# One evacuation path of an attention kernel: VectorE's two PSUM banks used one by one, batches of two units, and more than half of the integer shifts moved to GpSimd

## The chip, the cores and the metric

The kernel runs on one core of one Trainium2 chip. The metric is device time in microseconds (us) of one execution. The kernel before was timed at 739.3 us (median of three runs, 736.5 to 740.5).

Engine names in the profile: PE is TensorE (PEld its weight loads), ACT is ScalarE, DVE is VectorE, POOL is GpSimd, SP is the engine that issues most of the DMAs.

## The reference

Two attention blocks on the same input, mixed by a gate. Block A is softmax attention with 32 heads of 16 columns over 2048 positions; block B is linear attention.

```python
# B=1, S=2048, D=512, H=32, Dh=16
def _A_ref(x, wqkv, wo):
    q, k, v = ...                                    # (x @ wqkv), split in heads
    scores = jnp.einsum("bhqd,bhkd->bhqk", q, k) * (Dh ** -0.5)
    p = _softmax(scores, axis=-1)
    o = jnp.einsum("bhqk,bhkd->bhqd", p, v)
    return merge_heads(o) @ wo
g = sigmoid((x * gate_w).sum(-1, keepdims=True))
return g * _A_ref(x, A_wqkv, A_wo) + (1 - g) * _B_ref(x, B_wqkv, B_wo)
```

The cost is in A: 32 heads x 2048 x 2048 scores, each exponentiated once. In the kernel a *unit* is 128 keys x 512 queries of one head, and there are 2048 units to exponentiate (730 x 2 by ScalarE and 294 x 2 by VectorE in the kernel before).

## The kernel before

A scheduler written in Python lays out the instructions of all engines at build time, from a cost in nanoseconds that each operation is given. The order on each engine is then fixed. Engines are synchronised by semaphores where data demands it, and only there.

A unit's scores are exponentiated in one of two ways. ScalarE does it with one exponential for two units (128x1024). VectorE does it by arithmetic on the bits: it adds a constant to the scaled score, stores it as int16 (`op1`), and reads those bits as bfloat16, which is roughly a power of two. To be accurate enough it needs three such terms: the bits, the bits + 43 and the bits + 86 (`shift`), which TensorE sums with values scaled by three coefficients. TensorE's matmuls write to PSUM, here one tile, `ps`, of 4096 fp32 columns, which the kernel divides in eight banks of 512. Banks 0 to 3 hold scores for ScalarE, banks 4 and 5 those for VectorE, bank 7 the accumulator.

```python
SHIFTS = (0, 43, 86)
NPS, NZ, NQZ, NVQ = 10, 8, 3, 6
P = SB([128, NPS, 1024], BF16, "P")          # ScalarE's exponentials
Z = SB([128, NZ, 2048], I16, "Z")            # VectorE's, four units to a slot
# ... cut ...
def d_choose(start, late=0.0):               # may TensorE fill VectorE's banks now?
    if d_busy[0] or max(t_free(4), t_free(5)) > max(start + 30.0, late):
        return []                            # both banks have to be free
    # ... picks up to two units, for banks 4 and 5 ...

def cand_op1():                              # VectorE: both banks at once, 128x1024
    # ... cut ...
    return C(DV, 400, 533 * n + 74, lambda: nc.vector.tensor_scalar(o, i, ZB, 0.0, op0=ALU.add, op1=ALU.max), ...)

def cand_shift():                            # VectorE: four units at once, 128x2048
    # ... cut ...
    return C(DV, 300, 602, lambda: nc.vector.tensor_scalar(Z[:, z, :], Z[:, z0, :], float(m), None, op0=ALU.add), ...)

def cand_exp():                              # ScalarE: two units, 128x1024
    # ... cut ...
    return C(AC, 500, 427 * n + 49, lambda: nc.scalar.activation(P[:, slot, 0:512 * n], bank(b0, n), ACT.Exp, scale=ESC), ...)
```

GpSimd does small work. Its `tensor_scalar` operations are written so:

```python
# values times a coefficient, 32 times
nc.gpsimd.tensor_scalar(Vc[:, k, vs]..., Vc[:, 0, vs]..., COEF[k], 1.0, op0=ALU.mult, op1=ALU.mult)
# linear attention's feature map, 32 times each
nc.gpsimd.tensor_scalar(eb[:, i, :], eb[:, i, :], 1.0, 0.0, op0=ALU.min, op1=ALU.max)
nc.gpsimd.tensor_tensor(dst_ap, eb[:, i, :], mb[:, i, :], ALU.add)
# the gate, once each, on 64 columns
nc.gpsimd.tensor_scalar(ge[:], gt[:], 1.0, None, op0=ALU.add)                       # line 896
nc.gpsimd.tensor_scalar(ge[:], gt[:], -1.0, 1.0, op0=ALU.mult, op1=ALU.add)         # line 898
```

The main loop takes the candidate that can start first, appends it to its engine's list with the waits for its data (`emit`), and advances the planned clock.

The softmax here doesn't subtract the row's maximum and nothing guards it: scores larger than these inputs give would overflow.

Of the kernel before, what the change touches and what calls it, by code (L numbers as in the profile page):

```python
# [14 lines left out]
STATS = {}  # L15
# [110 lines left out]
def bass_gated_mix__mha_block__linear_attn_block__prompt_kernel(  # L126
# [31 lines left out]
    FILL = 0.65  # L158
    SLK = 0.0
# [3 lines left out]
    NPS, NZ, NQZ, NVQ = 10, 8, 3, 6  # L163

    with ExitStack() as es:
# [34 lines left out]
        Z = SB([128, NZ, 2048], I16, "Z")  # L200
# [225 lines left out]
        d_busy = [False]  # L426
# [71 lines left out]
        def d_batch():  # L498

            if dst["cur"] is None:  # L500
# [8 lines left out]
                dst["cur"] = {"todo": [0, 1, 2, 3], "z": z, "units": {}, "done": 0}  # L509
            return dst["cur"]  # L510

        def d_choose(start, late=0.0):

            if d_busy[0] or max(t_free(4), t_free(5)) > max(start + 30.0, late):
                return []
            cur = d_batch()
            if cur is None:
                return []
            js = sorted(cur["todo"], key=lambda j: (head(j), -len(uq[min(head(j), NR - 1)][j])))
            got = [(j, d_unit(j)) for j in js]  # L520
            got = sorted([x for x in got if x[1] is not None][:2])
            return [(cur, j, u, 4 + k) for k, (j, u) in enumerate(got)]
# [5 lines left out]
        class C:  # L528
            __slots__ = ("E", "prio", "dur", "fns", "reads", "writes", "after", "name", "mode", "wt")

            def __init__(self, E, prio, dur, fns, reads, writes, after, name, mode=None, wt=1.0):
                self.wt = wt
                self.E, self.prio, self.dur, self.fns = E, prio, dur, fns
                self.reads, self.writes, self.after, self.name, self.mode = reads, writes, after, name, mode

        def d_loaded(extra):
            for cur, j, u, bk in extra:
                r, kb = u
                take(r, kb, j)
                cur["todo"].remove(j)  # L540
                cur["units"][j] = u
                left[r][j] += NTERM - 1
                kb_left[(r, kb)] += NTERM - 1
            if extra:
                d_busy[0] = True
                dst["op1"].append((cur, [x[1] for x in extra]))
# [3 lines left out]
        def cand_s():  # L550
# [6 lines left out]
            extra = d_choose(start, s_window()[1] - SLK)  # L557
            units = act_pick(2, {x[1] for x in extra})
# [11 lines left out]
            def after(fin):  # L570
# [4 lines left out]
                STATS["sn"][nn] = STATS["sn"].get(nn, 0) + 1  # L575
                exps.append((sset, units))
# [20 lines left out]
        def cand_op1():  # L597
            if not dst["op1"]:
                return None
            cur, js = dst["op1"][0]  # L600
            z = cur["z"]
            n = len(js)

            def after(fin):
                dst["op1"].popleft()
                d_busy[0] = False
                cur["done"] += n
                d_finish(cur)
            zj = Z[:, z, :].rearrange("p (j c) -> p j c", j=4)
            o = zj[:, js[0]:js[1] + 1:js[1] - js[0], :] if n == 2 else zj[:, js[0], :]  # L610
            i = bank(4, 2).rearrange("p (j c) -> p j c", j=2) if n == 2 else bank(4)
            return C(DV, 400, 533 * n + 74, lambda: nc.vector.tensor_scalar(o, i, ZB, 0.0, op0=ALU.add, op1=ALU.max),  # L612
                     [r_bank[4 + k] for k in range(n)], [r_Z[z]], after, f"op1 {[cur['units'][j] + (j,) for j in js]}")

        def z_items(cur, z, term):
            for j, (r, kb) in cur["units"].items():
                def rel():
                    z_pend[z] -= 1
                add_item(r, kb, j, Z[:, z, 512 * j:512 * (j + 1)].bitcast(BF16), r_Z[z], rel, term, f"z{term}")

        def d_finish(cur):
            n = len(cur["units"])
            if cur["done"] < n or (cur["todo"] and any(d_unit(j) is not None for j in cur["todo"])) or cur.get("fin"):
                return
            if cur["todo"]:
                if any(head(j) < NR - 1 for j in cur["todo"]):
# [5 lines left out]
            z_pend[z] = n + NTERM - 1  # L632
            z_items(cur, z, 0)
# [3 lines left out]
        def cand_shift():  # L637
# [10 lines left out]
            cur, m, z0, kt = dst["shifts"][0]  # L648

            def after(fin):  # L650
# [3 lines left out]
                z_items(cur, z, kt)  # L654
            return C(DV, 300, 602, lambda: nc.vector.tensor_scalar(Z[:, z, :], Z[:, z0, :], float(m), None, op0=ALU.add),  # L655
                     [r_Z[z0]], [r_Z[z]], after, f"shift {m}")
# [708 lines left out]
```

## Time and profile before

| | before |
|---|---|
| span of the profiled run | 740.2 us |
| ScalarE busy | 697.7 us (94%), idle 42.5 |
| VectorE busy | 667.6 us (90%) |
| GpSimd busy | 128.3 us (17%) |
| granted TensorE clock | 0.977 |

The first line is the busy line of the page: us, share of the span, number of instructions.

```profile
PE 689.5 (93%) x6663; PEld 209.2 (28%) x6757; DVE 667.6 (90%) x813; ACT 697.7 (94%) x769; POOL 128.3 (17%) x184
```

These are groups of the page of the kernel before: line, engine, operation, tiles, shapes, count, then busy us and mean ns of one, then the idle time of the engine just before them and what ended it.

```profile
L677 ACT ACTIVATE P<-ps 128x1024 bf16<-128x1024 f32 x730 | 682.4, 1045 | 23.3 <-PE ps L331 22.1
L612 DVE TENSOR_SCALAR Z<-ps 128x1024 int16<-128x1024 f32 x294 | 357.2, 1215 | 42.8 <-PE ps L331 41.8
L655 DVE TENSOR_SCALAR Z<-Z 128x2048 int16<-128x2048 int16 x294 | 215.4, 750 | 3.0
...
L947 POOL TENSOR_SCALAR eb<-eb 128x512 f32<-128x512 f32 x32 | 23.1, 722 | 148.9 <-DVE mb L945 74.8
...
L876 POOL TENSOR_SCALAR Vc<-Vc 128x576 bf16<-128x576 bf16 x32 | 23.3, 727 | 88.6 <-DVE Vc L873 87.3
```

ScalarE's exponentials overlap (mean 1.045 us, but 682.4 / 730 = 0.935 us each), and it waits for TensorE only 22 us. The table by stretches of the span (columns: stretch, its length, then busy us of PE, PEld, DVE, ACT, POOL, then the granted clock and DMA) says that ScalarE is nearly full in the middle:

```profile
40.00:140.00 100.00, 94.25 (x908) 27.04 (x920) 95.70 (x119) 98.20 (x110) 23.27 (x31) 1.00 0.03 7
140.00:280.00 140.00, 131.33 (x1287) 39.18 (x1303) 130.49 (x152) 137.22 (x154) 31.36 (x40) 1.00 0.02 4
280.00:380.00 100.00, 96.85 (x961) 27.63 (x975) 91.94 (x112) 99.87 (x110) 7.54 (x14) 1.00 0.02 4
```

VectorE's shifts, in the view of one line's instructions (durations min/median/max in ns), are mostly alike, with a long tail:

```profile
L655 DVE TENSOR_SCALAR Z<-Z x294: 621/685/1754, 14.1 to 725.3; 128x2048 int16<-128x2048 int16 x147
```

And two lines of GpSimd's timeline (start us, duration us), the two gate operations quoted above.

```profile
67.72 0.87 POOL L896 TENSOR_SCALAR ge<-gt 128x64 f32<-128x64 f32 x1 [0.81 <-ACT gt L895]
69.26 0.24 POOL L898 TENSOR_SCALAR ge<-gt 128x64 f32<-128x64 f32 x1 [0.67 <-DVE gt L897]
```

The same 64 columns took 0.87 us with one operation and 0.24 us with two.

### The profile page before, as it was taken

What the parts mean: (1) busy time and instruction counts of PE and PEld (TensorE: products, weight loads), DVE (VectorE), ACT (ScalarE), POOL (GpSimd) and SP (SyncE); (2) the same over time, 40 slices, a digit from 0 to 9 for tenths busy, and PEclk for the clock granted to TensorE, in tenths of its full rate; (3) what the DMA queues carried; (4) which work ended last, traced back from release to release, by engine and by line L of the source; (5) the groups of instructions that cost most, each with busy time, mean ns of one, the idle gap of its engine ahead of it and who ended that gap; (6) DMA issues with size and microseconds to landing.
All of it is one profiled execution on the core that took longest, in us unless ns stands there. A gap on an engine that the chain in (4) does not pass through costs nothing.

```text
span 740.2 us, 16623 instructions
## 1 busy us (share of the span) xinstructions
PE 689.5 (93%) x6663; PEld 209.2 (28%) x6757; DVE 667.6 (90%) x813; ACT 697.7 (94%) x769; POOL 128.3 (17%) x184
## 2 busy tenths in 40 slices
PE   6999999899999999999999999999899989999997
PEld 2322222222323222222233322222233222222222
DVE  6799999998999999988897999999999968999894
ACT  4899999999999999999999999999999969999993
POOL 1301341212311220000010034233430000000000
PEclk8999999999999999999999999999999869999999
DMA  5900000000000000000000000000002021000001
GB/s 128 317 13 15 2 5 4 2 8 2 1 8 3 8 1 2 8 2 8 1 8 3 7 3 3 7 1 3 1 8 44 19 48 30 16 15 16 16 15 36
DMA packets 27836, 15.49 MB, mean 21 GB/s; under 512 B 19696, under 2 KB 26736, under 8 KB 27760
## 3 DMA queue, kind: packets, MB, share of 16 engines
q1 hardware_dynamic: 26704, 14.17, 7.0%
q8 instruction: 53, 0.87, 0.5%
q10 hardware_dynamic: 1056, 0.26, 0.2%
q14 instruction: 23, 0.19, 0.1%
HBM read 6.69 MB, written 2.10 MB: 12 GB/s over the span
## 4 chain that ended last, share of the span: by engine, by line
PE 58%; DVE 23%; ACT 9%; issue 7%; POOL 1%; DMA 0%; ACTq 0%; POOLq 0%; DVEq 0%
PE ps L331 58%; DVE Z L612 12%; ACT P L677 9%; DVE Z L655 6%; DVE mb L945 1%; DVE T L909 1%; DVE Vc L873 1%; DMA xnat<-wA 0%; DVE QT L845 0%; DVE OAT L936 0%; DVE KT L823 0%; ACT eb L944 0%; DVE wA L1032 0%; POOL Vc L876 0%; POOL phiK L948 0%
## 5 line engine op out<-in xcount | busy, mean ns | idle before, releaser
L677 ACT ACTIVATE P<-ps 128x1024 bf16<-128x1024 f32 x730 | 682.4, 1045 | 23.3 <-PE ps L331 22.1
L612 DVE TENSOR_SCALAR Z<-ps 128x1024 int16<-128x1024 f32 x294 | 357.2, 1215 | 42.8 <-PE ps L331 41.8
L331 PE MATMUL ps<-Qz,KT 32*128 32x512 bf16 x2048 | 291.3, 390 | 15.4 <-DVE Z L612 5.2
L331 PE MATMUL ps<-Z,Vc 128*17 128x512 bf16 x1764 | 227.8, 387 | 6.9 <-DVE Z L655 6.2
L655 DVE TENSOR_SCALAR Z<-Z 128x2048 int16<-128x2048 int16 x294 | 215.4, 750 | 3.0
L331 PE MATMUL ps<-P,Vc 128*17 128x512 bf16 x1460 | 204.0, 388 | 2.7 <-ACT P L677 0.9
L331 PEld LDWEIGHTS ps<-Qz,KT 32*128 32x128 bf16 x2048 | 73.7, 91 | 259.5 <-ACT P L677 182.5
L331 PEld LDWEIGHTS ps<-Z,Vc 128*17 128x17 bf16 x1764 | 52.1, 88 | 90.3 <-issue 45.2
L331 PE MATMUL ps<-warm 128*32 128x512 bf16 (+17 forms) x524 | 70.6, 334 | 3.8 <-issue 2.2
L331 PEld LDWEIGHTS ps<-P,Vc 128*17 128x17 bf16 x1460 | 47.3, 88 | 72.5 <-issue 35.4
L929 POOL TENSOR_TENSOR rg<-rec,gt 128x16 f32<-128x16 f32 x31 | 11.8, 380 | 297.2 <-DVE rec L916 297.2
L947 POOL TENSOR_SCALAR eb<-eb 128x512 f32<-128x512 f32 x32 | 23.1, 722 | 148.9 <-DVE mb L945 74.8
L948 POOL TENSOR_TENSOR phiK<-eb,mb 128x512 bf16<-128x512 f32 x32 | 43.2, 1350 | 2.3
L876 POOL TENSOR_SCALAR Vc<-Vc 128x576 bf16<-128x576 bf16 x32 | 23.3, 727 | 88.6 <-DVE Vc L873 87.3
L331 PE MATMUL ps<-xT,wA 128*128 128x512 bf16 x105 | 33.5, 388 | 5.1 <-issue 3.1
L909 DVE STREAM_TRANSPOSE T<-ps 128x512 f32<-128x512 f32 x32 | 22.6, 707 | 9.3 <-PE ps L331 9.3
L331 PEld LDWEIGHTS ps<-warm 128*32 128x32 bf16 (+1 forms) x541 | 20.6, 95 | 23.9 <-issue 17.9
L945 DVE TENSOR_SCALAR mb<-ps 128x512 f32<-128x512 f32 x32 | 21.6, 677 | 1.3 <-PE ps L331 0.9
L331 PE MATMUL ps<-wA,xT 128*128 128x128 bf16 x256 | 21.8, 226 | 0.6 <-DVE KT L823 0.2
L944 ACT ACTIVATE eb<-ps 128x512 f32<-128x512 f32 x32 | 20.0, 624 | 0.6 <-PE ps L331 0.6
L932 POOL TENSOR_TENSOR T<-T,rg 128x256 bf16<-128x256 f32 x31 | 19.6, 632 | 2.4
L331 PE MATMUL ps<-woA,OAT 128*128 128x512 bf16 x55 | 16.6, 382 | 2.2 <-DVE OAT L924 1.2
(76 smaller groups left out, 247.0 us busy)
## 6 DMA issues: line engine op xcount, KB each, us to landing
Qz<-QT SPq DMA_DIRECT2D x120, 16.0 KB, 1.8
wA<-in_A_wqkv_dram SPq DMA_DIRECT2D x1, 1536.0 KB, 8.4
wB<-in_B_wqkv_dram SPq DMA_DIRECT2D x1, 1536.0 KB, 11.8
xnat<-in_A_x_dram SPq DMA_DIRECT2D x3, 512.0 KB, 12.7
out_dram<-outt SPq DMA_DIRECT2D x12, 128.0 KB, 1.7
xnat<-in_A_x_dram SPq DMA_DIRECT2D x4, 128.0 KB, 3.3
woA<-in_A_wo_dram SPq DMA_DIRECT2D x1, 512.0 KB, 8.7
woB<-in_B_wo_dram SPq DMA_DIRECT2D x1, 512.0 KB, 9.3
```

Source lines behind the costliest of these rows:

```text
L331: return lambda: nc.tensor.matmul(o, lhsT=l, rhs=r, start=start, stop=stop, skip_group_check=sg)
L612: return C(DV, 400, 533 * n + 74, lambda: nc.vector.tensor_scalar(o, i, ZB, 0.0, op0=ALU.add, op1=ALU.max), [r_bank[4 + k] for k in range( ...
L655: return C(DV, 300, 602, lambda: nc.vector.tensor_scalar(Z[:, z, :], Z[:, z0, :], float(m), None, op0=ALU.add), [r_Z[z0]], [r_Z[z]], after ...
L677: return C(AC, 500, 427 * n + 49, lambda: nc.scalar.activation(P[:, slot, 0:512 * n], bank(b0, n), ACT.Exp, scale=ESC), [r_bank[b0 + k] fo ...
L876: yield po(750, lambda k=k: nc.gpsimd.tensor_scalar(Vc[:, k, vs].rearrange("p a b c -> p (a b c)"), Vc[:, 0, vs].rearrange("p a b c -> p ( ...
L909: yield dv(607, lambda: nc.vector.transpose(T1[:, a, :], bank(7)), [r_bank[7]], [r_T1[a]])
L929: yield po(250, lambda: nc.gpsimd.tensor_tensor(rg[:, a, :], rec[:, a, :], gt[:, qc, :], ALU.mult), [r_rec[a], r_gt], [r_rg[a]])
L932: yield po(800, lambda: nc.gpsimd.tensor_tensor(t2[:, :, 16 * par:16 * par + 16], t1[:, :, 0:16], rg[:, a, :].unsqueeze(2).to_broadcast([1 ...
L944: yield ac(480, lambda: nc.scalar.activation(eb[:, i, :], bank(b), ACT.Exp), [r_bank[b]], [r_eb[i]])
L945: yield dv(607, lambda: nc.vector.tensor_scalar(mb[:, i, :], bank(b), 0.0, 1e-6, op0=ALU.max, op1=ALU.add), [r_bank[b], r_eb[i]], [r_mb[i]])
L947: yield po(700, lambda: nc.gpsimd.tensor_scalar(eb[:, i, :], eb[:, i, :], 1.0, 0.0, op0=ALU.min, op1=ALU.max), [r_eb[i]], [r_eb[i]])
L948: yield po(1300, lambda: nc.gpsimd.tensor_tensor(dst_ap, eb[:, i, :], mb[:, i, :], ALU.add), [r_eb[i], r_mb[i]], dst_res)
```

## The change

Intent: give VectorE's way more of the units, so that ScalarE has less to do. VectorE's banks 4 and 5 become free one at a time, a batch (and so a shift) is two units instead of four, and a shift may be done by either VectorE or GpSimd. The change takes it that a VectorE shift and a GpSimd instruction exclude each other, at what its scheduler calls the port and treats as a resource that an operation with `lock` holds. The traces show that such a shift waits while a GpSimd instruction runs, not what lies behind it; "port" (or "shared port") is only the name for it below. In the trace before, the shifts that began with 0.9 to 1.3 us of a GpSimd instruction left took 1.62 us in the median (9 of the 294), those that met none 0.685 us (219). Of the numbers at the top, `FILL` sets how much filler (matmuls that only keep TensorE busy) is laid in, `SLK` by how many ns earlier VectorE's banks have to be free to be filled, `PMIN` how many shifts have to be queued before GpSimd takes one, `PLATE` by how many ns GpSimd may be free later than VectorE and still take it, and `HOT` how near its end a round has to be for its shifts to go first.

```diff
-    FILL = 0.65
-    SLK = 0.0
+    FILL = 0.75
+    HOT = 24
+    SHB = 2
+    PMIN = 2
+    PLATE = 0.0
+    SLK = 120.0
...
-    NPS, NZ, NQZ, NVQ = 10, 8, 3, 6
+    NB = 2
+    NPS, NZ, NQZ, NVQ = 10, 16, 3, 6
...
-        Z = SB([128, NZ, 2048], I16, "Z")
+        Z = SB([128, NZ, 512 * NB], I16, "Z")
...
-            if d_busy[0] or max(t_free(4), t_free(5)) > max(start + 30.0, late):
+            banks = [b for b in (4, 5) if not d_busy[b] and t_free(b) <= max(start + 30.0, late)]
+            if not banks:
                 return []
...
+                self.lock = lock or E is PO
...
-        def cand_shift():
+        def cand_pshift():
+            return cand_shift(PO)
+
+        def cand_shift(E=DV):
...
+            if E is PO and (len(dst["shifts"]) < PMIN or PO.free > DV.free + PLATE):
+                return None
...
-            return C(DV, 300, 602, lambda: nc.vector.tensor_scalar(Z[:, z, :], Z[:, z0, :], float(m), None, op0=ALU.add),
+            if E is PO:
+                return C(PO, 400, 300 + 412 * n, lambda: nc.gpsimd.tensor_scalar(Z[:, z, 0:512 * n], Z[:, z0, 0:512 * n], float(m), None, op0=ALU.add),
+                         [r_Z[z0]], [r_Z[z]], after, f"pshift {m}")
+            ...
+            return C(DV, 450 if hot else 300, 69 + 134 * n, lambda: nc.vector.tensor_scalar(Z[:, z, 0:512 * n], Z[:, z0, 0:512 * n], float(m), None, op0=ALU.add),
+                     [r_Z[z0]], [r_Z[z]], after, f"shift {m}", lock=True)
...
+                if c.lock:
+                    start = max(start, port["pool" if c.E is DV else "dve"])
...
+            if c.lock:
+                c.E.free = max(c.E.free, start)
+                port[c.E.name] = start + c.dur + 20.0
```

The scheduler's cost of a GpSimd shift of 1024 columns (n = 2) is 300 + 824 = 1124 ns.

More of the change, by code (lines that the diff above doesn't have):

```diff
@@ L157, in bass_gated_mix__mha_block__linear_attn_block__prompt_kernel @@
     SWITCH = 100.0
-    FILL = 0.65
-    SLK = 0.0
+    FILL = 0.75
+    HOT = 24
+    BACK = 600.0
+    SHB = 2
+    why = [None]
+    PMIN = 2
+    PLATE = 0.0
+    SLK = 120.0
     DSL = 300.0
     STICK = 450.0
-    NPS, NZ, NQZ, NVQ = 10, 8, 3, 6
+    NB = 2
+    NPS, NZ, NQZ, NVQ = 10, 16, 3, 6
     with ExitStack() as es:
@@ L425, in bass_gated_mix__mha_block__linear_attn_block__prompt_kernel @@
         owner = {6: None}
-        d_busy = [False]
+        dcnt = [[0] * 4 for _ in range(NR)]
+        d_busy = {4: False, 5: False}
         kb_left = {(r, kb): 4 for r in range(NR) for kb in range(NKB)}
@@ L508, in d_batch @@
                 dst["open"] += 1
-                dst["cur"] = {"todo": [0, 1, 2, 3], "z": z, "units": {}, "done": 0}
+                dst["cur"] = {"todo": NB, "z": z, "units": [], "done": 0}
             return dst["cur"]
         def d_choose(start, late=0.0):
-            if d_busy[0] or max(t_free(4), t_free(5)) > max(start + 30.0, late):
+            banks = [b for b in (4, 5) if not d_busy[b] and t_free(b) <= max(start + 30.0, late)]
+            if not banks:
+                why[0] = "busy" if any(d_busy[b] for b in (4, 5)) else "late"
                 return []
@@ L517, in d_choose @@
             if cur is None:
+                why[0] = "noZ"
                 return []
-            js = sorted(cur["todo"], key=lambda j: (head(j), -len(uq[min(head(j), NR - 1)][j])))
-            got = [(j, d_unit(j)) for j in js]
-            got = sorted([x for x in got if x[1] is not None][:2])
-            return [(cur, j, u, 4 + k) for k, (j, u) in enumerate(got)]
+            got = [(j, d_unit(j)) for j in range(4)]
+            got = sorted([x for x in got if x[1] is not None], key=lambda x: (x[1][0], dcnt[x[1][0]][x[0]], -len(uq[x[1][0]][x[0]])))
+            got = sorted(got[:min(len(banks) if len(dst["op1"]) < 1 and DV.free < start + BACK and len(dst["shifts"]) < SHB else 1, cur["todo"])])
+            why[0] = "none" if not got else "ok"
+            return [(cur, j, u, b) for b, (j, u) in zip(banks, got)]
         def add_item(r, kb, j, ap, res, rel, term, name):
@@ L528, in bass_gated_mix__mha_block__linear_attn_block__prompt_kernel, with __init__ @@
         class C:
-            __slots__ = ("E", "prio", "dur", "fns", "reads", "writes", "after", "name", "mode", "wt")
-            def __init__(self, E, prio, dur, fns, reads, writes, after, name, mode=None, wt=1.0):
+            __slots__ = ("E", "prio", "dur", "fns", "reads", "writes", "after", "name", "mode", "wt", "lock")
+            def __init__(self, E, prio, dur, fns, reads, writes, after, name, mode=None, wt=1.0, lock=False):
                 self.wt = wt
+                self.lock = lock or E is PO
                 self.E, self.prio, self.dur, self.fns = E, prio, dur, fns
@@ L539, in d_loaded @@
                 take(r, kb, j)
-                cur["todo"].remove(j)
-                cur["units"][j] = u
+                cur["todo"] -= 1
+                cur["units"].append((r, kb, j))
+                dcnt[r][j] += 1
                 left[r][j] += NTERM - 1
@@ L544, in d_loaded @@
             if extra:
-                d_busy[0] = True
-                dst["op1"].append((cur, [x[1] for x in extra]))
+                for x in extra:
+                    d_busy[x[3]] = True
+                for k, x in enumerate(extra):
+                    dst["op1"].append((cur, len(cur["units"]) - len(extra) + k, [x[3]]))
                 if not cur["todo"]:
@@ L557, in cand_s @@
             extra = d_choose(start, s_window()[1] - SLK)
+            w = why[0]
             units = act_pick(2, {x[1] for x in extra})
@@ L575, in after @@
                 STATS["sn"][nn] = STATS["sn"].get(nn, 0) + 1
+                STATS.setdefault("why", {})
+                STATS["why"][w] = STATS["why"].get(w, 0) + 1
                 exps.append((sset, units))
@@ L599, in cand_op1, with z_items @@
                 return None
-            cur, js = dst["op1"][0]
+            cur, k0, bks = dst["op1"][0]
             z = cur["z"]
-            n = len(js)
+            n = len(bks)
             def after(fin):
                 dst["op1"].popleft()
-                d_busy[0] = False
+                for b in bks:
+                    d_busy[b] = False
+                z_items(cur, z, 0, range(k0, k0 + n))
+                z_pend[z] += n
                 cur["done"] += n
                 d_finish(cur)
-            zj = Z[:, z, :].rearrange("p (j c) -> p j c", j=4)
-            o = zj[:, js[0]:js[1] + 1:js[1] - js[0], :] if n == 2 else zj[:, js[0], :]
-            i = bank(4, 2).rearrange("p (j c) -> p j c", j=2) if n == 2 else bank(4)
+            o = Z[:, z, 512 * k0:512 * (k0 + n)]
+            i = bank(bks[0], n)
             return C(DV, 400, 533 * n + 74, lambda: nc.vector.tensor_scalar(o, i, ZB, 0.0, op0=ALU.add, op1=ALU.max),
-                     [r_bank[4 + k] for k in range(n)], [r_Z[z]], after, f"op1 {[cur['units'][j] + (j,) for j in js]}")
-        def z_items(cur, z, term):
-            for j, (r, kb) in cur["units"].items():
+                     [r_bank[b] for b in bks], [r_Z[z]], after, f"op1 {cur['units'][k0:k0 + n]}")
+        def z_items(cur, z, term, ks):
+            for k in ks:
+                r, kb, j = cur["units"][k]
                 def rel():
                     z_pend[z] -= 1
-                add_item(r, kb, j, Z[:, z, 512 * j:512 * (j + 1)].bitcast(BF16), r_Z[z], rel, term, f"z{term}")
+                add_item(r, kb, j, Z[:, z, 512 * k:512 * (k + 1)].bitcast(BF16), r_Z[z], rel, term, f"z{term}")
         def d_finish(cur):
             n = len(cur["units"])
-            if cur["done"] < n or (cur["todo"] and any(d_unit(j) is not None for j in cur["todo"])) or cur.get("fin"):
+            if cur["done"] < n or (cur["todo"] and any(d_unit(j) is not None for j in range(4))) or cur.get("fin"):
                 return
             if cur["todo"]:
-                if any(head(j) < NR - 1 for j in cur["todo"]):
+                if any(head(j) < NR - 1 for j in range(4)):
                     return
@@ L631, in d_finish @@
             dst["open"] -= 1
-            z_pend[z] = n + NTERM - 1
-            z_items(cur, z, 0)
+            z_pend[z] += NTERM - 2
             for k, m in enumerate(SHIFTS[1:]):
                 dst["shifts"].append((cur, m, z, k + 1))
-        def cand_shift():
+        def cand_pshift():
+            return cand_shift(PO)
+        def cand_shift(E=DV):
             if dst["cur"] is not None and dst["cur"]["todo"]:
@@ L648, in cand_shift @@
             cur, m, z0, kt = dst["shifts"][0]
+            n = len(cur["units"])
+            if E is PO and (len(dst["shifts"]) < PMIN or PO.free > DV.free + PLATE):
+                return None
             def after(fin):
@@ L653, in after @@
                 z_pend[z0] -= 1
-                z_items(cur, z, kt)
-            return C(DV, 300, 602, lambda: nc.vector.tensor_scalar(Z[:, z, :], Z[:, z0, :], float(m), None, op0=ALU.add),
-                     [r_Z[z0]], [r_Z[z]], after, f"shift {m}")
+                z_items(cur, z, kt, range(len(cur["units"])))
+                STATS["sh" + E.name] = STATS.get("sh" + E.name, 0) + 1
+            if E is PO:
+                return C(PO, 400, 300 + 412 * n, lambda: nc.gpsimd.tensor_scalar(Z[:, z, 0:512 * n], Z[:, z0, 0:512 * n], float(m), None, op0=ALU.add),
+                         [r_Z[z0]], [r_Z[z]], after, f"pshift {m}")
+            pr = st["pv_round"]
+            hot = pr < NR and sum(left[pr]) < HOT and any(u[0] <= pr for u in cur["units"])
+            return C(DV, 450 if hot else 300, 69 + 134 * n, lambda: nc.vector.tensor_scalar(Z[:, z, 0:512 * n], Z[:, z0, 0:512 * n], float(m), None, op0=ALU.add),
+                     [r_Z[z0]], [r_Z[z]], after, f"shift {m}", lock=True)
         def cand_exp():
@@ L1227, in fill_one @@
             t0 = PE.free + (SWITCH if m == "row" else 0.0)
-            free = [7] + [b for b in owner if owner[b] is None] + ([] if d_busy[0] or 4 in owner else [5, 4])
+            free = [7] + [b for b in owner if owner[b] is None] + [b for b in (5, 4) if b not in owner and not d_busy[b]]
             free = [b for b in free if _avail(PE, [], [r_bank[b]]) <= t0]
@@ L1249, in bass_gated_mix__mha_block__linear_attn_block__prompt_kernel @@
         guard = 0
+        port = {"pool": 0.0, "dve": 0.0}
         while True:
@@ L1257, in bass_gated_mix__mha_block__linear_attn_block__prompt_kernel @@
             cands = cand_tasks()
-            for f in (cand_s, cand_dsolo, cand_pv, cand_op1, cand_shift, cand_exp):
+            for f in (cand_s, cand_dsolo, cand_pv, cand_op1, cand_shift, cand_pshift, cand_exp):
                 c = f()
@@ L1272, in bass_gated_mix__mha_block__linear_attn_block__prompt_kernel @@
                     start = max(start, PE.free + SWITCH)
+                if c.lock:
+                    start = max(start, port["pool" if c.E is DV else "dve"])
+                    start0 = max(start0, start)
                 if c.E is PE and c.prio < 1000:
@@ L1279, in bass_gated_mix__mha_block__linear_attn_block__prompt_kernel @@
                     by[c.E] = (key, start, c)
-            key, start, c = min(by.values(), key=lambda v: v[1])
+            key, start, c = min(by.values(), key=lambda v: v[1] - (80.0 if v[2].E is DV and v[2].lock else 0.0))
             if c.E is PE:
```

## The prediction

> **What bounds the kernel now.** ScalarE, over most of the span. By the stretch table it is busy 98.2 of 100 us (40 to 140), 137.2 of 140, 99.9 of 100, 137.0 of 140. Its idle time is 740.2 - 697.7 = 42.5 us: about 20 in ramp and tail, the rest mostly waits of the exponential for TensorE (22.1 us in the list of waits). The groups give 730 exponentials in 682.4 us, 0.935 us each. VectorE (90% busy) is second: 294 evictions 128x1024 (1.14 us apart in the timeline) and 294 shifts 128x2048 (0.61 us apart; median 0.685, mean 0.75) beside about 100 us of other work. TensorE's 93% includes fillers and pipeline latency; that the chain that ended last gives it 58% says little, because it stands between the others at each hand-over. GpSimd is 17% busy.
>
> **What the change does**, counted from the instruction order of both builds.
> - ScalarE: 730 -> 711 exponentials, 19 x 0.935 = -18 us. VectorE's way takes 626 score units for 588.
> - VectorE evictions: 294 of 1024 become 626 of 512. Other 512-wide PSUM reads come 0.61 us apart, so 382 us for 335: +47.
> - VectorE shifts: 294 of 2048 become 266 of 1024, estimated at 0.34 us[...]: 91 us for 179, -88.
> - GpSimd: 360 new shifts of 1024, estimated at 1.1 us from 512 fp32 columns in 0.61 and 576 bf16 columns in 0.67: +400 us, to about 70% of the span.
> - TensorE: 3300 value matmuls for 3224; more filler; clock 0.977 -> about 0.98.
>
> **The cost against it.** [...]shifts take 0.62 to 1.75 us, the mean 65 ns over the median at 17% GpSimd load. [...]The new scheduler treats the port as a resource, so I expect 30 to 60, mean VectorE shift 0.5 to 0.65 us. VectorE's busy time then stays near today's (640 to 680 us). Separately released banks hide part of it: TensorE refills one while VectorE reads the other.
>
> **On the critical path**: only the 18 us of ScalarE, plus or minus the change in its idle time. VectorE stalls reach ScalarE only where TensorE's in-order queue stands before an unfreed bank or a missing shift. I expect ScalarE's idle time at 38 to 50 us: fewer waits for bank pairs, some new ones from port stalls, a tail 1 to 2 us longer (five final blocks for four).
>
> **Prediction: 723 us**, 8 in 10 between 707 and 739. Faster by over 2%: 0.54; within 2%: 0.40; slower by over 2%: 0.06.
>
> **What would show it.** Right: ScalarE about 680 us busy and over 95% in the middle; eviction group 626 x about 0.68 us; GpSimd 65 to 75% busy, its shift about 1.1 us; VectorE shifts widely spread (0.4 to 1.5 us). Wrong: GpSimd's int16 shift at 1.5 us or more, GpSimd 90% busy and TensorE waiting for it; VectorE shifts over 0.8 us on average, VectorE over 93% busy; ScalarE's wait for TensorE well over 30 us.
>
> **What would make it wrong.** Above the range: port stalls that the static order did not foresee make VectorE late, and everything is in order behind it. Below: single-bank release removes most ScalarE waits in the 520 to 700 us stretch.

The sum of this forecast, 681 us of ScalarE's work and about 42 us of its idle time, came to 723 us. The 0.34 us and the 30 to 60 us (of VectorE's stalls) stand as estimates; measured in mult_add were 0.335 us (three shifts in a row take 1.09 us at 316.39 us, the last 0.42 of them) and 54 us. In the 93% of TensorE there are 70.6 us of fillers, and its matmuls overlap: 2048 score matmuls of 390 ns each add 291.3 us to its busy time.

## The result, and the profile after

The changed kernel takes 1218.6 us (median of 4 runs, 1217.1 to 1223.6). The ratio to before is 1.649 (95% interval 1.642 to 1.657). Ratios here and below are the mean time of one kernel's fast runs over that of the other's of the same rounds, so not quite the ratio of the medians quoted.

The busy line of the page after, and two rows of its 40 slices (each digit tenths of a slice; PEclk is the granted TensorE clock):

```profile
PE 912.3 (75%) x7035; PEld 228.0 (19%) x7035; DVE 713.2 (59%) x1117; ACT 719.9 (59%) x750; POOL 1113.4 (92%) x544
...
POOL 3889999999979799999899999999999997899994
PEclk7867866787787788766766557698875658766778
```

GpSimd is the busy engine now, and the clock that TensorE is granted fell from 0.98 to 0.74. The chain of work that ended last, by engine and by line, goes through GpSimd's shift:

```profile
POOL 63%; issue 16%; PE 15%; DVE 5%; POOLq 0%; ACT 0%; ACTq 0%; DVEq 0%
POOL Z L685 59%; PE ps L338 15%; DVE Z L633 2%; DVE Z L689 2%; POOL Vc L910 1%; POOL phiK L982 1%; POOL T L966 1%; POOL eb L981 0%; POOL rg L963 0%; DVE T L943 0%; DVE mb L979 0%; PE ps L833 0%; DVE Qz L873 0%; POOL wA L1054 0%; DVE OAT L958 0%
```

The groups that answer to those shown of before:

```profile
L685 POOL TENSOR_SCALAR Z<-Z 128x1024 int16<-128x1024 int16 x360 | 999.2, 2800 | 65.4 <-DVE Z L633 60.3
L711 ACT ACTIVATE P<-ps 128x1024 bf16<-128x1024 f32 x711 | 702.5, 1025 | 470.3 <-PE ps L338 467.5
L633 DVE TENSOR_SCALAR Z<-ps 128x512 int16<-128x512 f32 x626 | 425.7, 685 | 419.4 <-PE ps L338 411.4
...
L689 DVE TENSOR_SCALAR Z<-Z 128x1024 int16<-128x1024 int16 x266 | 187.2, 738 | 0.4
...
L910 POOL TENSOR_SCALAR Vc<-Vc 128x576 bf16<-128x576 bf16 x32 | 21.9, 684 | 6.6 <-DVE Vc L907 4.3
...
L981 POOL TENSOR_SCALAR eb<-eb 128x512 f32<-128x512 f32 x32 | 20.3, 636 | 3.8 <-DVE mb L979 1.0
```

A GpSimd shift takes 2.8 us, 2.5 times the 1.12 us it was planned with; the other GpSimd operations take about what they took or a little less (0.68 us for 0.73, 0.64 for 0.72). 360 x 2.8 us is 999 us by itself. With the rest of GpSimd's work that is 1113 us, and 102 us of waits make the span. From the list of waits (waiter, what it waited for: us in total, times, longest):

```profile
ACT P L711 <- PE ps L338: 467.5, 384, 5.8
...
PEld ps L338 <- POOL Z L685: 325.7, 198, 4.7
PE ps L338 <- POOL Z L685: 268.5, 188, 4.2
```

TensorE, in order, stands at a value matmul whose shift GpSimd has not finished, and ScalarE's next scores stand behind it: at 305.70 us, for one, a value matmul begins after 2.20 us of waiting for GpSimd's shift, the next score matmuls at 306.25, and ScalarE's exponential at 306.68 after 2.12 us of waiting for them. ScalarE's wait for TensorE rose from 22 to 468 us. The same stretches as before show that ScalarE is no longer full (in the stretches not shown it is busy for 73% at most):

```profile
40.00:140.00 100.00, 71.70 (x547) 17.49 (x551) 55.55 (x91) 56.07 (x60) 93.10 (x52) 0.74 0.02 5
140.00:280.00 140.00, 107.14 (x815) 24.55 (x807) 79.58 (x123) 84.86 (x90) 136.50 (x66) 0.73 0.01 3
```

The lower clock (a score matmul takes 483 ns on average where it took 390) is a consequence: with TensorE's instructions in the same order and only the form of the GpSimd shift different (in ma_order the waits too), the granted clock was 0.65 in two_op below (TensorE 64% busy), 0.74 here (75%), 0.96 in mult_add (94%) and 0.98 in ma_order (95%). Over this trace it is either full or half: 1.00 from 22.0 to 23.5 us, for instance, and 0.50 from 25 to 30. The runs show that the clock goes with TensorE's busy share, not what sets it.

The two gate operations, in the timeline after, are the clue:

```profile
100.34 0.37 POOL L930 TENSOR_SCALAR ge<-gt 128x64 f32<-128x64 f32 x1
...
103.63 0.24 POOL L932 TENSOR_SCALAR ge<-gt 128x64 f32<-128x64 f32 x1
```

0.37 us with one operation, 0.24 with two: 124 ns (368 less 244 in the view by line) on 64 columns, or 1.9 ns a column, which on 1024 columns would be an estimated 2.0 us, a little over the 1.7 us that are missing (2.80 less 1.12).

### The profile page after: what moved, and what is told of

Read it like the earlier page. It is cut to its first block, busy times and chain, and to the rows that moved or that the text cites. A ratio compares the mean times of both kernels' runs of the same rounds, so it can differ in the third digit from the quotient of the medians.

```text
span 1215.3 us, 18610 instructions
## 1 busy us (share of the span) xinstructions
PE 912.3 (75%) x7035; PEld 228.0 (19%) x7035; DVE 713.2 (59%) x1117; ACT 719.9 (59%) x750; POOL 1113.4 (92%) x544
## 4 chain that ended last, share of the span: by engine, by line
POOL 63%; issue 16%; PE 15%; DVE 5%; POOLq 0%; ACT 0%; ACTq 0%; DVEq 0%
POOL Z L685 59%; PE ps L338 15%; DVE Z L633 2%; DVE Z L689 2%; POOL Vc L910 1%; POOL phiK L982 1%; POOL T L966 1%; POOL eb L981 0%; POOL rg L963 0%; DVE T L943 0%; DVE mb L979 0%; PE ps L833 0%; DVE Qz L873 0%; POOL wA L1054 0%; DVE OAT L958 0%
## 5 line engine op out<-in xcount | busy, mean ns | idle before, releaser
L685 POOL TENSOR_SCALAR Z<-Z 128x1024 int16<-128x1024 int16 x360 | 999.2, 2800 | 65.4 <-DVE Z L633 60.3
L633 DVE TENSOR_SCALAR Z<-ps 128x512 int16<-128x512 f32 x626 | 425.7, 685 | 419.4 <-PE ps L338 411.4
L338 PE MATMUL ps<-Z,Vc 128*17 128x512 bf16 x1878 | 357.2, 487 | 179.9 <-POOL Z L685 167.6
L338 PE MATMUL ps<-P,Vc 128*17 128x512 bf16 x1422 | 327.9, 488 | 105.5 <-POOL Z L685 100.9
L338 PE MATMUL ps<-Qz,KT 32*128 32x512 bf16 x2048 | 346.7, 483 | 10.8 <-DVE Z L633 4.5
L689 DVE TENSOR_SCALAR Z<-Z 128x1024 int16<-128x1024 int16 x266 | 187.2, 738 | 0.4
L338 PE MATMUL ps<-warm 128*32 128x512 bf16 (+13 forms) x743 | 99.2, 394 | 1.4 <-POOL warm L380 1.4
L338 PE MATMUL ps<-phiK,xnat 128*128 128x512 bf16 x64 | 25.8, 495 | 0.0
L338 PE MATMUL ps<-woB,xnat 128*128 128x512 bf16 x64 | 24.4, 485 | 0.0
L338 PE MATMUL ps<-wB,xT 128*128 128x512 bf16 x64 | 24.1, 466 | 0.0
```

What stands on the lines that cost most here:

```text
L338: return lambda: nc.tensor.matmul(o, lhsT=l, rhs=r, start=start, stop=stop, skip_group_check=sg)
L685: return C(PO, 400, 300 + 412 * n, lambda: nc.gpsimd.tensor_scalar(Z[:, z, 0:512 * n], Z[:, z0, 0:512 * n], float(m), None, op0=ALU.add), ...
L689: return C(DV, 450 if hot else 300, 69 + 134 * n, lambda: nc.vector.tensor_scalar(Z[:, z, 0:512 * n], Z[:, z0, 0:512 * n], float(m), None, ...
```

## The experiments

The first question was why a GpSimd shift takes 2.8 us. My theory F: it is the form, one operation in place of two. Rivals: T, it is the type, int16; P, VectorE holds the shared port.

### bench: the instruction by itself

The kernel before, with GpSimd instructions appended after the tiles' last use, each form twice.

```diff
+            lambda: G(zj, zi, 43.0, None, op0=ALU.add),                               # L1309, int16, 1024
+            lambda: G(zj, zi, 43.0, 0.0, op0=ALU.add, op1=ALU.add),                   # L1310
+            lambda: G(zj[:, 0:512], zi[:, 0:512], 43.0, None, op0=ALU.add),           # L1311
+            lambda: G(zj[:, 0:512], zi[:, 0:512], 43.0, 0.0, op0=ALU.add, op1=ALU.add),
+            lambda: G(pj, pi, 2.0, None, op0=ALU.mult),                               # L1313, bf16
+            lambda: G(pj, pi, 2.0, 1.0, op0=ALU.mult, op1=ALU.mult),                  # L1314
+            lambda: G(fj, fi, 1.0, None, op0=ALU.add),                                # L1315, fp32
+            lambda: G(fj, fi, 1.0, 0.0, op0=ALU.add, op1=ALU.add),
+            lambda: G(zj, zi, 43.0, None, op0=ALU.add),
+            lambda: G(zj, zi, 43.0, 0.0, op0=ALU.add, op1=ALU.max),
```

> The kernel before with twenty GpSimd instructions appended after its last use of the tiles, when VectorE is idle: each form twice, on 1024 (or 512) columns. Theory F (form): a tensor_scalar on GpSimd with one operation is slow and the same with two operations is fast, whatever the type: int16 1024 one-op 2.77 us, two-op about 1.1; bf16 and fp32 likewise one-op 2.7, two-op 1.1. Theory T (type): int16 is slow in both forms (2.77 and 2.77 or more), bf16 and fp32 are near 1.1 in both. Theory P (port): the operation is slow in the changed kernel because VectorE holds the shared port; then every form here, with VectorE idle, takes about 1.1. The span grows by the appended work, 20 to 60 us.

GpSimd's timeline, two instructions to a line:

```profile
733.99 5.62 POOL L1309 TENSOR_SCALAR Z<-Z 128x1024 int16<-128x1024 int16 x2 [23.36 <-DVE T L921]
739.69 7.35 POOL L1310 TENSOR_SCALAR Z<-Z 128x1024 int16<-128x1024 int16 x2
747.12 3.06 POOL L1311 TENSOR_SCALAR Z<-Z 128x512 int16<-128x512 int16 x2
...
754.29 5.64 POOL L1313 TENSOR_SCALAR P<-P 128x1024 bf16<-128x1024 bf16 x2
760.01 2.18 POOL L1314 TENSOR_SCALAR P<-P 128x1024 bf16<-128x1024 bf16 x2
762.27 5.63 POOL L1315 TENSOR_SCALAR eb<-T 128x1024 f32<-128x1024 f32 x2
```

One operation takes 2.77 us in int16, bf16 and fp32 alike, with VectorE idle: T and P fall. But F as I had put it falls too. Two operations, add and add, take 3.63 us, more than one. Only mult with mult is fast, 1.05 us. The durations agree with the spacing: two in a row take 5.62 us, which is twice 2.77 and a gap of 0.08, and the pair after them begins at 739.69, 5.70 us after the first.

### two_op: theory F in the kernel

```diff
- nc.gpsimd.tensor_scalar(Z[:, z, 0:512 * n], Z[:, z0, 0:512 * n], float(m), None, op0=ALU.add)
+ nc.gpsimd.tensor_scalar(Z[:, z, 0:512 * n], Z[:, z0, 0:512 * n], float(m), 0.0, op0=ALU.add, op1=ALU.add)
```

> The changed kernel with one edit: the GpSimd shift adds 0.0 as a second operation; the order of instructions on every engine and the result are unchanged. Theory F: the shift falls from 2.77 to about 1.1 us, GpSimd to about 45 to 75% busy, ScalarE's wait for TensorE from 467 us to under 40, the granted clock back to 0.97 or more, time 710 to 740 us. Theories T and P: nothing changes, 2.77 us and 1218 us.

```profile
L685 POOL TENSOR_SCALAR Z<-Z 128x1024 int16<-128x1024 int16 x360 | 1306.0, 3654 | 65.1 <-DVE Z L633 60.0
```

1521.4 us (ratio to before 2.057): my repair made it 303 us slower. The shift took 3.65 us; 360 x (3.65 - 2.80) = 306 us. So the time follows GpSimd's shift one for one, as it must where GpSimd is the bound. A miss as a repair, but it shows the slope.

### dve_only: the banks and batches without GpSimd

```diff
-    HOT = 24
-    PMIN = 2
+    HOT = 48
+    PMIN = 10 ** 6
```

> The changed kernel with no shift on GpSimd (all 578 on VectorE, in batches of 1024) and the priority limit HOT raised from 24 to 48, without which the schedule does not close; 578 evictions of 512, 735 exponentials. If GpSimd's shift is the whole cause, the banks used one by one and the small batches do no harm of that kind: ScalarE 735 x 0.935 + 16 = 703 us busy, time 735 to 765 us. If the banks or batches are a part of the cause, over 800 us.

```profile
L711 ACT ACTIVATE P<-ps 128x1024 bf16<-128x1024 f32 x735 | 687.8, 1050 | 21.8 <-PE ps L338 20.5
...
L689 DVE TENSOR_SCALAR Z<-Z 128x1024 int16<-128x1024 int16 x578 | 230.7, 441 | 1.6
```

744.9 us, ratio 1.0074 (1.0055 to 1.0092). The banks used one by one and the batches of two do no harm by themselves. ScalarE is idle for 743.4 - 703.7 = 39.7 us, as before (42.5); it has 735 exponentials where before had 730, and 5 x 0.935 us is most of the 5 us lost.

### true_cost: the slow instruction, honestly planned

```diff
- return C(PO, 400, 300 + 412 * n, ...
+ return C(PO, 400, 2800 / 2 * n, ...
```

> The changed kernel, one-op shift kept, but the scheduler is told 2.8 us for a GpSimd shift of 1024 in place of 1.12; it then plans 156 shifts on GpSimd, 384 on VectorE, 754 exponentials. If the loss came of a slow instruction AND an order planned for a fast one, a right plan loses little: 754 x 0.935 + 16 = 721 us of ScalarE, time 755 to 800 us. If a 2.8 us GpSimd instruction is ruinous in itself (it shuts VectorE's shifts out of the port), VectorE shifts rise above 1 us on average and the time stays over 850 us.

805.8 us, a little over my range, ratio 1.090. Most of the 479 us are avoided when the plan knows the cost: it is the slow instruction and an order planned for a fast one together that cost so much. VectorE's shift was 0.64 us on average, so a slow GpSimd instruction does not shut VectorE out as I had feared (more on this below).

### bench2: which pairs are fast

> The kernel before with another list of GpSimd tensor_scalar forms appended, each twice, VectorE idle. The first list showed 2.77 us for one operation and 3.63 for add with add or max, in int16 and fp32 alike, against 1.05 for mult with mult in bf16. Theory S (special pairs): GpSimd is fast only for certain pairs of operations, and mult-then-add is one of them (the kernel's own mult-add on 64 columns took 0.24 us, its one-op add on 64 columns 0.37 in the changed kernel): int16 mult-add, mult-mult and min-max take 1.0 to 1.1 us, add-first pairs 3.6. Theory D (bf16 only): the fast case was fast because of bf16: int16 and fp32 mult-add take 3.6 us, bf16 mult-add 1.05.

The same appended list, with other pairs. Two instructions to a line again; after each line number of the fence I name the form below.

```profile
733.90 2.17 POOL L1309 TENSOR_SCALAR Z<-Z 128x1024 int16<-128x1024 int16 x2 [23.37 <-DVE T L921]
...
739.81 2.16 POOL L1312 TENSOR_SCALAR Z<-Z 128x1024 int16<-128x1024 int16 x2
742.05 2.17 POOL L1313 TENSOR_SCALAR Z<-Z 128x1024 int16<-128x1024 int16 x2
744.31 7.34 POOL L1314 TENSOR_SCALAR Z<-Z 128x1024 int16<-128x1024 int16 x2
...
768.83 2.17 POOL L1318 TENSOR_SCALAR eb<-T 128x1024 f32<-128x1024 f32 x2
771.09 5.62 POOL L1319 TENSOR_SCALAR Z<-Z 128x1024 int16<-128x1024 int16 x2
```

L1309 is int16 mult then add, L1312 min then max, L1313 add then mult, L1314 max then add, L1318 fp32 mult then add, L1319 a single max. Of both lists:

| form on 128x1024 | one instruction |
|---|---|
| mult-mult, mult-add, add-mult, min-max; any type tried | 1.04 us |
| one operation (add, mult or max) | 2.77 us |
| add-add, add-max, add-min, max-add, mult-max | 3.63 us |
| copy | 1.04 us |

Theory S holds, except that add-first is not always slow: add-mult is fast. On 512 columns the three kinds take 0.62, 1.49 and 1.93 us; the difference over 512 columns gives 0.83, 2.50 and 3.33 ns a column. What the pairs have in common on the inside no run shows.

### mult_add: the change with the fast form

```diff
- nc.gpsimd.tensor_scalar(Z[...], Z[...], float(m), None, op0=ALU.add)
+ nc.gpsimd.tensor_scalar(Z[...], Z[...], 1.0, float(m), op0=ALU.mult, op1=ALU.add)
```

> The changed kernel with the GpSimd shift written as mult by 1.0, then add, in place of add alone; same values, same order of instructions on every engine. Theory S: the shift takes 1.05 to 1.15 us, GpSimd about 70% busy, granted clock 0.97 or more, ScalarE 681 us busy, time 712 to 735 us. Theory D: 3.6 us a shift and 1520 us. If the shift is fast and the time still over 745 us, the shared port or the order is a second cost.

757.2 us. The shift takes 1.06 us and 461 of the 479 us are gone; the order on every engine is that of the changed kernel. So the form of one instruction is shown to be the main cause. Yet the ratio is 1.020 (1.017 to 1.024), where I had predicted a gain. ScalarE's work is near the prediction (688.4 us busy, about 680 predicted), its idle time is not: 757.1 - 688.4 = 68.7 us for 42.5.

```profile
L711 ACT ACTIVATE P<-ps 128x1024 bf16<-128x1024 f32 x711 | 672.5, 1037 | 48.1 <-PE ps L338 45.8
...
L685 POOL TENSOR_SCALAR Z<-Z 128x1024 int16<-128x1024 int16 x360 | 383.1, 1064 | 143.3 <-DVE Z L633 115.6
...
L689 DVE TENSOR_SCALAR Z<-Z 128x1024 int16<-128x1024 int16 x266 | 155.8, 621 | 0.4
```

VectorE's shift has a median of 0.42 us and a mean of 0.62. 266 x 0.20 = 54 us of stalls. VectorE's evictions, which read PSUM, do not stall: 0.683 us on average here and 0.681 in dve_only.

The second question, then: is what is left the shared port, or the finer pieces, SLK, or GpSimd's results coming late in front of TensorE?

### port_before and port_dve: traffic at the port, nothing else

Orders unchanged; GpSimd instructions that nothing depends on are added, each after a VectorE instruction.

```diff
+ PO.add(lambda: nc.gpsimd.tensor_scalar(scr[:], scr[:], 1.0, 0.0, op0=ALU.mult, op1=ALU.add),
+        [_Ev(DV, DV.n), _Ev(PO, PO.n)])      # scr: 128x768, one byte a column
```

> The kernel before, every engine's order unchanged except that 443 GpSimd instructions that nothing depends on (a fast mult-add on 768 one-byte columns of a scratch tile, estimated 0.83 us each) are strewn along its length, each released by a VectorE instruction. They bring GpSimd to about 65% busy, as in the kernel with the fast shift. Theory P (the shared port is what is left of the loss): VectorE's shift of 2048 rises from 0.75 to 0.95 us or more on average, with no other duration changed, and the time rises by 1 to 5%. Rival O (what is left comes of the new order and the shorter pieces, the port is harmless): time within 0.5% of before.

> The version with all shifts on VectorE (744.9 us), order unchanged, with 441 such GpSimd instructions added. Its 578 VectorE shifts meet the port twice as often as in the kernel with the fast shift (266), where the mean shift rose from 0.44 to 0.62 us. Theory P: mean shift 0.55 us or more, VectorE over 95% busy in the middle, time up by 20 to 100 us (765 to 845). Rival O: 742 to 752 us.

828.2 us (ratio 1.118) and 874.5 us (1.182). VectorE's shift rose from 0.75 to 0.93 us and from 0.44 to 0.61 us on average: 54 and 95 us more stall in all, for 88 and 130 us more time. (An added instruction took 0.83 us, as estimated: midway between mult-add's 0.62 on 512 columns and 1.04 on 1024.) The port matters. The losses are larger than the stalls, and larger than I expected, for the added instructions also delay GpSimd's real work (ScalarE waited 14.4 us for `phiK` in the first), so the two runs are not a clean measure of the port.

### ma_slk0 and ma_plate: two knobs

Both are the fast-shift kernel with one number changed: `SLK = 0.0`, and `PLATE = -600.0`.

> The kernel with the fast shift (757 us) and SLK back at 0, as before the change: 708 exponentials, 379 shifts on GpSimd, 253 on VectorE. If the larger SLK is one of the losses, 735 to 745 us; under the port theory it changes little, 750 to 762 us.

> The kernel with the fast shift, but GpSimd takes a shift only where it would be free 0.6 us before VectorE: 288 shifts on GpSimd (360), 336 on VectorE (266), 712 exponentials. Fewer GpSimd instructions, more VectorE ones to collide: under the port theory about the same, 745 to 765 us. If GpSimd's latency in front of TensorE is what is left, faster: 725 to 742 us.

765.8 us (four runs, 763.5 to 773.2), above both of my ranges, with a VectorE shift of 0.74 us on average; and 754.5 us (three fast runs, ratio 1.020). Neither number is a cause: the first is slower, the second equal. The 288 GpSimd shifts of the second, in place of 360, gave nothing back, because 336 VectorE shifts met the port (mean 0.60 us, free 0.42).

### ma_half: shorter holds

```diff
- lambda: nc.gpsimd.tensor_scalar(Z[:, z, 0:512 * n], Z[:, z0, 0:512 * n], 1.0, float(m), ...)
+ [lambda k=k: nc.gpsimd.tensor_scalar(Z[:, z, 512 * k:512 * k + 512], Z[:, z0, 512 * k:512 * k + 512], 1.0, float(m), ...) for k in range(n)]
```

> The kernel with the fast shift (757.2 us; VectorE's shift 0.62 us on average), same order, but each GpSimd shift of 1024 is two of 512 columns (0.62 us each in the list of forms): GpSimd's busy time rises from 499 to about 590 us, but it holds the port for 0.62 us at a time in place of 1.05. Port theory: VectorE waits for at most one piece, its mean shift falls to 0.50 to 0.57 us, and the time falls by 3 to 12 us in spite of the slower GpSimd. Rival (GpSimd's results come late in front of TensorE): the time rises by 5 us or more.

770.4 us (five fast runs), slower by 13 us. VectorE's shift fell only to 0.605 us on average, and its median rose from 0.420 to 0.463: the stalls are shorter and there are more of them. A GpSimd piece took 0.62 us, the whole shift 1.05. GpSimd rose to 577 us, and TensorE's waits for GpSimd's shift rose from 10 to 66 us. Neither theory gains by this run alone; the version had both costs.

### ma_nolock: a plan that knows no port

```diff
- self.lock = lock or E is PO
+ self.lock = False
```

> The kernel with the fast shift, planned by a scheduler that does not know of the shared port (the resource taken out): 701 exponentials, 270 shifts on GpSimd, 378 on VectorE. Its ScalarE work is 701 x 0.935 + 16 = 671 us. Port theory: its stalls are not planned for; mean VectorE shift 0.65 us or more, VectorE over 92% busy, ScalarE idle for 90 us or more, time 760 to 790 us. Rival: if the port does not matter, it gains by its fewer exponentials: 735 to 750 us.

763.6 us (ratio 1.033), with ScalarE idle for 76.8 us, less than the 90 I had said. VectorE's shift was 0.61 us over 378 shifts. The plan with the port as a resource gains 6 us over this; it does not remove the stalls.

### pool_only: no shift on VectorE

```diff
- PMIN = 2
+ PMIN = 1
+ if len(dst['shifts']) >= 2 or PO.free > start + 2000.0:
+     return []
- if E is PO and (len(dst["shifts"]) < PMIN or PO.free > DV.free + PLATE):
+ if E is DV or len(dst["shifts"]) < PMIN:
```

> All 496 shifts on GpSimd in the fast form, none on VectorE, so no VectorE operation here should need the shared port often; score units are given to VectorE only while GpSimd keeps up (776 exponentials). ScalarE has 776 x 0.935 + 16 = 742 us of work. Port theory: ScalarE's idle time is back to the 40 us of the kernel before and of the version with all shifts on VectorE: 775 to 790 us. Rival (banks, small batches or the wait for GpSimd cost it): idle 65 us or more, 805 us and up.

```profile
PE 738.3 (95%) x7035; PEld 225.9 (29%) x7138; DVE 463.3 (60%) x721; ACT 740.0 (96%) x815; POOL 633.5 (82%) x680
...
L713 ACT ACTIVATE P<-ps 128x1024 bf16<-128x1024 f32 x776 | 724.9, 1048 | 14.7 <-PE ps L338 13.6
```

775.9 us, with more exponentials (776), but ScalarE is idle for only 773.4 - 740.0 = 33.4 us. With GpSimd busy for 82% of the span, VectorE's evictions took 0.687 us (0.681 in dve_only), its transposes 0.709 and its `mb` operations 0.685 (0.707 and 0.683 there): they do not stall. Banks one by one, batches of two and waits for GpSimd are all in this version. So the two versions in which only one engine shifts leave ScalarE idle for 33 and 40 us, the mixed one for 69. That points to the port, though pool_only also leaves VectorE with less to do (60% busy); dve_only does not (93%).

### ma_order and ma_order2: the planned order at the port, enforced

The plan decides who takes the port first, but nothing in the program holds the engines to it: no data links a VectorE shift with the GpSimd instruction planned after it. If VectorE is a little late, GpSimd starts first and VectorE's shift stalls (in mult_add for 1.26 us in place of 0.42 where 0.9 to 1.3 us of GpSimd's instruction were left), with the evictions, and so TensorE's banks, behind it. The first version adds a semaphore wait to each GpSimd instruction, for the VectorE shift planned before it; the second also the reverse. Instructions and orders are the same on all engines as in mult_add.

```diff
+                if c.lock and c.E is PO and port_ev["dve"]:
+                    xdeps.append(port_ev["dve"])
                 fin = emit(c.E, c.dur, c.fns, c.reads, c.writes, name=c.name)      # deps_of(...) + xdeps
+                xdeps.clear()
+                if c.lock:
+                    port_ev[c.E.name] = _Ev(c.E, c.E.n)
```

> The kernel with the fast shift (757.2 us), same instructions in the same order on every engine, and one kind of wait more: each GpSimd instruction waits for the VectorE shift that the plan put before it, so that a GpSimd instruction planned later cannot take the port first. Port theory: VectorE's shift falls from 0.62 to 0.45 to 0.55 us on average, ScalarE's idle time from 69 to about 50 us, time 735 to 750 us; GpSimd has the slack to wait. Rival (the port stalls are not what keeps ScalarE idle): shift shorter, time unchanged (752 to 762 us).

> The same, and also the other way: each VectorE shift waits for the GpSimd instruction planned before it, so the port is taken in the planned order by both. A shift that waits at a semaphore is not counted as busy, so its mean should be near the free 0.42 us, but VectorE then waits for late GpSimd work: time between 740 and 775 us; slower than the one-way version if GpSimd runs late against the plan, the same if it does not.

```profile
PE 679.4 (95%) x6945; PEld 209.3 (29%) x7035; DVE 625.8 (88%) x1117; ACT 678.5 (95%) x750; POOL 489.8 (69%) x544
...
L714 ACT ACTIVATE P<-ps 128x1024 bf16<-128x1024 f32 x711 | 663.3, 1053 | 13.8 <-PE ps L341 13.1
...
L692 DVE TENSOR_SCALAR Z<-Z 128x1024 int16<-128x1024 int16 x266 | 108.9, 445 | 0.4
```

712.4 us (710.3 to 714.5), ratio to before 0.961 (0.957 to 0.965), from 757.2 by waits alone, and better than I expected. The shift's mean fell from 0.621 to 0.445 us, ScalarE's wait for TensorE from 45.8 to 13.1 us, its idle time to 712.4 - 678.5 = 33.9 us. In mult_add 97 of the 266 VectorE shifts began with more than 0.2 us of a GpSimd instruction left, here 29. GpSimd had the slack for it: its shifts waited 50 us for VectorE's. With the wait both ways it is 720.8 us (0.973): the shift is 0.42 us, but VectorE now waits for GpSimd work that runs late. With the controls below this settles the second cause: the order in which the two engines take the port.

### before_order, slow_order and mo_slk0: controls

before_order is the kernel before with the same one-way wait; slow_order is ma_order with the change's one-operation add; mo_slk0 is ma_order with `SLK = 0.0`.

> The kernel before, same orders, with the same kind of wait: each GpSimd instruction waits for the VectorE shift planned before it. Before has 184 GpSimd instructions and 65 ns of port stall on each of 294 shifts, 19 us in all. If the gain of 45 us is owed to the mixed plan's port stalls, there is little to gain here: 732 to 742 us. If the waits help by something else, 725 us or less.

> The kernel with the enforced port order (712.4 us), but with the change's own one-operation add as the GpSimd shift (2.77 us). 360 x 2.77 + 125 = 1122 us of GpSimd alone; the form of the instruction is then the bound and the order cannot help: 1190 to 1260 us, GpSimd over 88% busy.

> The kernel with the enforced port order and SLK back at 0 (708 exponentials, 379 shifts on GpSimd). Without the order this plan was 8 us slower than its sibling (765.8 against 757.2); with it ScalarE's 708 exponentials are 3 us less work: 705 to 716 us.

742.4 us, ratio 0.9995: the old kernel gains nothing by the order, so the gain of ma_order is not the wait alone but the change with its two faults mended. 1233.5 us, ratio 1.663: with the slow form the order cannot help; its shift took 2.79 us and GpSimd was 90% busy. 712.6 us, ratio 0.960: the same as ma_order, and the 8 us by which this plan was slower without the order are gone.

## Why the prediction was wrong

- **What bounds the kernel before: ScalarE.** The runs bear it out. In each version with few stalls the time is ScalarE's work plus 33 to 43 us: before 697.7 + 42.5, dve_only 703.7 + 39.7, pool_only 740.0 + 33.4, ma_order 678.5 + 33.9.
- **The counts and VectorE's durations**: right. 626 evictions at 0.685 us (about 0.68 predicted); shifts that follow one another in mult_add 0.335 us apart (0.34 predicted; each lasts 0.42 us in the median).
- **The step that failed**: "GpSimd: 360 new shifts of 1024, estimated at 1.1 us from 512 fp32 columns in 0.61 and 576 bf16 columns in 0.67: +400 us, to about 70% of the span." It took 2.80 us each, 999 us in all. The estimate carried a duration over from min-max and mult-mult to a single add, as if only columns counted. The list of forms shows that the pair of operations decides, by a factor of 2.7 to 3.5, and the type does not. The prediction did name a slow int16 shift as what would show it wrong, but gave no reason for it and almost no weight (6% for slower). The trace of before held a hint in two lines, 0.87 us for a single add on 64 columns and 0.24 us for mult-add, but a blurred one: about 0.5 us of the 0.87 is not the form, for the same instruction took 0.37 us in the kernel after, where no VectorE shift ran beside it.
- **The port's cost**: "30 to 60" us of VectorE stalls, right in size where the shift is fast (54 us in mult_add); with the slow form it was 266 x (0.738 - 0.418) = 85 us.
- **A second step that failed, hidden by the first**: "I expect ScalarE's idle time at 38 to 50 us". With the fast form it was 68.7. I took it that separately released banks would hide part of the 54 us of stalls. But 26 us more of idle time than before reached ScalarE (68.7 less 42.5), and with the stalls taken away 35 us of idle time went (68.7 less 33.9), because everything is in order behind VectorE and the planned order at the port is not kept in the run (97 of the 266 VectorE shifts of mult_add began with more than 0.2 us of a GpSimd instruction left). The prediction had named this as what would take it above its range. With the order enforced the idle time is 33.9 us, below my range.
- **The sum**: 681 us of ScalarE work and about 42 idle gave 723. With both faults mended the kernel takes 712.4 us, so the gain that the change was made for was there, 28 us: 19 of ScalarE's work (697.7 less 678.5) and 9 of its idle time.

## What to carry to other kernels

Cost an instruction by its exact form, operations included, from a run of that form; a second operation that changes nothing may be what makes it fast (1.04 us for mult then add on 128x1024, 2.77 for one add) or slow (3.63 for add then add). When two engines share a resource that a plan reserves, the reservation is only a wish unless a semaphore enforces it: let the engine that has slack wait for the one that does not (757.2 us without that wait, 712.4 with it). When an order is fixed at build time, one instruction that is slower than planned can cost many times what it would cost an order that knew of it (1218.6 against 805.8 us here, a loss of 479 against 66).

## How long a VectorE shift waits for a GpSimd instruction

These were taken from the traces by laying each VectorE shift over the GpSimd instruction running when it began.

- GpSimd instructions of 1.05 us: in mult_add, VectorE shifts that began with 0.9 to 1.3 us of one left took 1.26 us in the median (32 shifts), 0.42 free. They waited for the rest of it.
- The 2.77 us form: in the changed kernel, the 82 shifts that began with 1.3 to 2.0 us of it left took 0.416 us in the median and 0.485 at most, as if the port were free, while the 25 that began with 0.9 to 1.3 us left took 1.25 us, and the 54 that began with more than 2.0 us left 1.12. The same holds in true_cost: 84 shifts that began with 1.3 to 2.0 us left took 0.437 at most. So this form makes a shift wait near its beginning and near its end, and not between.
